# Recurrent attention and a squareplus layer: logarithms one group ahead, separate second-layer banks, crossbar transposes for row blocks 12 to 23

## Chip, cores and metric

The kernel runs on one core of a Trainium2 chip. The metric is the device time of one execution in microseconds (us). Engines are named as in the profile: PE (TensorE), DVE (VectorE), ACT (ScalarE), POOL (GpSimd) and SP, whose queue issues the DMAs here.

## What is computed

A gated linear attention with 4 batches, 8 heads, 768 steps and 48 features a head, followed by a two-layer network with 384 inputs and 2048 hidden units over the 3072 tokens:

```python
f = 1.0 / (1.0 + np.exp(-f_logit))
for t in range(S):
    state = f[:, :, t, :, None] * state + np.einsum('bhd,bhe->bhde', k[:, :, t], v[:, :, t])
    y[:, :, t] = np.einsum('bhd,bhde->bhe', q[:, :, t], state)
x = y.transpose(0, 2, 1, 3).reshape(B * S, H * D)
h = x @ w_in
g = 0.5 * (h + np.sqrt(h * h + 4.0))
out = g @ w_out
```

All inputs and the output are float32.

## The kernel before

**Units.** The 768 steps of a batch are six chunks of 128, so there are 24 *row blocks* of 128 tokens. Two row blocks make a *pair* (12 pairs), the unit of loading and of the first layer. `GROUPS` (L18) joins pairs to *groups* of 1, 1, 1, 2, 3, 3 and 1 pairs.

**Loads.** `load_pair` (L96) issues eight DMAs of 192 KB on SP for a pair: two row blocks each of f_logit, q, k and v. Each of the four kinds has four buffers, so a load waits until the pair four before it has been used up. The weights come in eight DMAs of 768 KB (L113, L119) and are cast to fp16 on ACT (w_in) and DVE (w_out).

**The window of a group** (`window`, L125) turns logits into scaled q and k. `exp_ln` (L131): ACT computes ln(1+exp(-f)) in two passes (L134, L135), DVE splits it into an fp16 part `lhi` (L137) and an fp16 remainder `llo` (L138), POOL casts v (L140). There are two buffers of lhi and llo. `cums` (L143): PE multiplies lhi and llo with a triangular matrix into the banks `hps` (L148, L149), ACT takes the exponentials `ea` and `eap` (L155, L156), POOL multiplies q and k by them into fp16 `qt` and `kt` (L157, L158), PE sums over half chunks (L164, L165), and DVE copies these sums to `nls` (L166). `gammas` (L168): DVE adds neighbouring sums to `gi` (L180), and ACT takes the decay from chunk to chunk, `gam` (L183). `run_window` (L366) puts an activation table load before and after this (exp and ln on one side, square root on the other).

**Attention of a row block**, in steps: `st_T` (L201) transposes q and k on PE, eight 128x128 tiles into a bank `tr`, and DVE copies them to `qkT` (L208). `st_SC` (L211) forms the scores of 8 heads in two banks and masks them on DVE (`pm`, L220). `st_KV` (L224) updates the state (`sn`, L235). `st_Y` (L239) forms y, which DVE casts (L251). `st_YT` (L254) transposes y on PE, three tiles, and DVE copies it into the pair's `xT` (L261). `attention` (L264) lays the steps of a group out in slots: transposes of its i-th row block in slot 4i, scores in 4i+2, state in 4i+3, y in 4i+5, y transposed in 4i+8.

**The two layers.** `mlp1` of a pair (L288) has eight halves of twelve matmuls (two by 256 columns, L299 six at a time) into the four `hps` banks; after every second half ACT squares (L306) and takes the root (L307), and DVE writes g (L310). `mlp2` (L317) has eight *quarters* of four matmuls (L328) into a bank `o`; after the fourth, DVE copies o to `o_sb` (two buffers, L332) and SP stores it (L334).

**Order.** ACT keeps the program's order. On the other engines a compile-time scheduler picks, by its own model of time, what is ready, earlier instructions in the program first; at run time every engine is in order. `run_mlp1` (L376) spreads the slots of attention over the halves, and takes quarters of the second layer from the list `fill` only when no slots are left or the list is longer than 24. `run_window` takes two quarters after each of its steps. The window of a group stands before mlp1 of the group before it.

**PSUM.** Four banks `hps`, and a pool of four, `pp_a`, that attention and o share.

Of the kernel before, what the change touches and what calls it, by code (L numbers as in the profile page):

```python
# [8 lines left out]
FP32 = mybir.dt.float32  # L9
# [5 lines left out]

GROUPS = [(0, 2), (2, 4), (4, 6), (6, 10), (10, 16), (16, 22), (22, 24)]  # L18
# [3 lines left out]
def kernel(  # L22
# [10 lines left out]
    nc = tc.nc  # L33
# [23 lines left out]
    pp_a = ctx.enter_context(tc.tile_pool(name="pp_a", bufs=4, space=PSUM))  # L57
# [20 lines left out]
    qt = [konst.tile([128, PR, H, 64], FP16, name=f"qt{i}") for i in range(NB)]  # L78
    kt = [konst.tile([128, PR, H, 64], FP16, name=f"kt{i}") for i in range(NB)]
    lhi = [konst.tile([128, PR, H, 64], FP16, name=f"lhi{i}") for i in range(2)]  # L80
    llo = [konst.tile([128, PR, H, 64], FP16, name=f"llo{i}") for i in range(2)]
# [14 lines left out]
    def load_pair(p):  # L96
        got = {}
        for name, src in (("f", f_logit), ("q", q), ("k", k), ("v", v)):
            t = ldp.tile([128, PR, H, D], FP32, name=f"ld_{name}", tag=f"ld_{name}")
            got[name] = t  # L100
        for name, src in (("f", f_logit), ("q", q), ("k", k), ("v", v)):
            for r in range(PR):
                b, c = divmod(p * PR + r, NC)
                nc.sync.dma_start(out=got[name][:, r],  # L104
                                  in_=src[b][:, c * C:(c + 1) * C, :].rearrange("h t d -> t h d"))
        loads[p] = got
# [18 lines left out]
    def window(g):  # L125

        r0, r1 = GROUPS[g]
        pairs = range(r0 // PR, r1 // PR)
        lss, steps = {}, []

        def exp_ln(p):  # L131
            f = loads[p]["f"]
            ls = wp.tile([128, PR, H, D], FP32, name="ls", tag="ls")
            nc.scalar.activation(out=f, in_=f, func=AF.Exp, scale=-1.0)  # L134
            nc.scalar.activation(out=ls, in_=f, func=AF.Ln, bias=1.0, scale=1.0)  # L135
            hi, lo = lhi[p % 2], llo[p % 2]
            nc.vector.tensor_copy(out=hi[:, :, :, 0:D], in_=ls)  # L137
            nc.vector.tensor_tensor(out=lo[:, :, :, 0:D], in0=ls, in1=hi[:, :, :, 0:D], op=ALU.subtract)  # L138
            v16 = bp.tile([128, PR, H, D], FP16, name="v16", tag="v16", bufs=4)
            nc.gpsimd.tensor_copy(out=v16, in_=loads[p]["v"])  # L140
            v16s[p] = v16

        def cums(p):  # L143
            hi, lo = lhi[p % 2], llo[p % 2]
            hp2 = [hps[2 * (p % 2) + r] for r in range(PR)]
            for r in range(PR):
                ca = hp2[r][:, 0:H * D]
                nc.tensor.matmul(out=ca, lhsT=wcent, rhs=hi[:, r, :, 0:D], start=True, stop=False)  # L148
                nc.tensor.matmul(out=ca, lhsT=wcent, rhs=lo[:, r, :, 0:D], start=False, stop=True)  # L149
            ea = wp.tile([128, PR, H, D], FP32, name="ea", tag="ea")  # L150
            eap = wp.tile([128, PR, H, D], FP32, name="eap", tag="eap")
            ld = loads[p]
            for r in range(PR):
                ca = hp2[r][:, 0:H * D]
                nc.scalar.activation(out=ea[:, r].rearrange("p h d -> p (h d)"), in_=ca, func=AF.Exp, scale=-1.0)  # L155
                nc.scalar.activation(out=eap[:, r].rearrange("p h d -> p (h d)"), in_=ca, func=AF.Exp, scale=1.0)  # L156
            nc.gpsimd.tensor_tensor(out=qt[p % NB][:, :, :, 0:D], in0=ld["q"], in1=ea, op=ALU.mult)  # L157
            nc.gpsimd.tensor_tensor(out=kt[p % NB][:, :, :, 0:D], in0=ld["k"], in1=eap, op=ALU.mult)  # L158
            b, c = divmod(p * PR, NC)
            for r in range(PR):  # L160
                nl = hp2[r][:, H * D:H * D + 2 * NP].rearrange("p (j s) -> p j s", s=2)
                for hp in range(NP):
                    o = nl[:, hp, :]
                    nc.tensor.matmul(out=o, lhsT=hi[:, r, 2 * hp:2 * hp + 2, :], rhs=hvec, start=True, stop=False)  # L164
                    nc.tensor.matmul(out=o, lhsT=lo[:, r, 2 * hp:2 * hp + 2, :], rhs=hvec, start=False, stop=True)  # L165
                nc.vector.tensor_copy(out=nls[b % 2][:, c + r], in_=nl)  # L166

        def gammas():  # L168

            a = r0  # L170
            while a < r1:
                b, c = divmod(a, NC)
                e = min(r1, (b + 1) * NC)
                n = e - a
                nb, gm = nls[b % 2], gam[b % 2]
                c0 = max(c - 1, 0)
                c1 = c + n - 1
                if c1 > c0:
                    gi = wp.tile([128, NC, NP], FP32, name="gi", tag="gi")
# [9 lines left out]
        for i, p in enumerate(ps):  # L189
            if i + 1 < len(ps):  # L190
                steps.append(lambda p=ps[i + 1]: exp_ln(p))
            steps.append(lambda p=p: cums(p))
# [260 lines left out]
```

## Time and profile before

| | |
|---|---|
| median of 3 runs | 272.44 us (270.02 to 272.85) |
| profiled execution, its own time | 270.39 us |
| its span, first to last instruction | 268.6 us |
| mean granted PE clock | 0.929 |
| DMA, all queues | 30.22 MB in 107032 packets, of which 100352 are under 512 B |
| POOL busy | 57.5 us |

The span is what the trace covers; the 1.8 us to the execution's own time lie outside it. "Busy" counts an engine's instructions and not its waits. Matmuls overlap, so the busy time of PE is more than its work. A line of the timeline reads: start, length, engine, line of the code, operation, output<-inputs, and in brackets the idle time before it and what ended that. In the table of stages each row is one stretch of the span. Numbers after the bar in a group's row are its busy time, the mean ns of one instruction, and idle time with its releaser.

### The profile page before, as it was taken

The page shows a single profiled execution, that of the slowest core. Times are in us where ns is not written, and L with a number is a line of the kernel's source. Part 1 is how long each engine was busy: PE and PEld are TensorE (multiplying, and loading weights), DVE is VectorE, ACT ScalarE, POOL GpSimd, SP SyncE. Part 2 cuts the span into 40 slices and gives each one's busy share as a digit, 9 for nine tenths or more (in the row PEclk, how much of TensorE's full clock was granted, in tenths as well). Part 3 has the DMA queues.
Part 4 walks back from the last instruction along what each step waited for, and adds up shares of the span by engine and source line. Part 5 has one row for each costly group of instructions (what it writes and reads, how often), then busy time and mean ns, then how long its engine had stood idle before and what let it go on. Part 6 is the DMA issues. An engine that isn't in the chain of part 4 may idle for free.

```text
span 268.6 us, 5160 instructions
## 1 busy us (share of the span) xinstructions
PE 213.1 (79%) x2024; PEld 148.9 (55%) x2024; DVE 182.7 (68%) x332; ACT 169.3 (63%) x252; POOL 57.5 (21%) x52
## 2 busy tenths in 40 slices
PE   0366939897688775986886869999886999999995
PEld 0143626664446553575664537777654777767652
DVE  1456726863583899579999666999983697645521
ACT  4355567884822956548968645988867795938200
POOL 4325001004209001494110396000005000000000
PEclk9999995999555997999999989999998899999999
DMA  8995599599995099999994000000000000010121
GB/s 144 187 220 184 161 234 302 153 245 188 177 216 93 8 214 185 187 217 195 166 199 76 31 32 29 2 0 4 2 29 29 2 29 33 29 59 32 59 79 70
DMA packets 107032, 30.22 MB, mean 113 GB/s; under 512 B 100352, under 2 KB 105472, under 8 KB 107008
## 3 DMA queue, kind: packets, MB, share of 16 engines
q1 hardware_dynamic: 107008, 29.89, 58.8%
q8 instruction: 16, 0.26, 0.4%
q14 instruction: 8, 0.07, 0.1%
HBM read 25.17 MB, written 4.72 MB: 111 GB/s over the span
## 4 chain that ended last, share of the span: by engine, by line
PE 32%; DVE 22%; ACT 16%; DMA 10%; issue 8%; SPq 6%; POOL 4%; POOLq 1%; ACTq 0%; DVEq 0%
PE o L328 16%; PE hps L299 10%; SPq L104 6%; DVE g L310 6%; ACT hsq L306 4%; DVE pm L220 3%; ACT r L307 3%; DMA ld_v<-in_v_dram 3%; DMA ld_f<-in_f_logit_dram 3%; DMA w_st<-in_moe_w_in_dram 3%; DVE qkT L208 2%; DVE llo L138 2%; POOL kt L158 2%; DVE y L251 2%; ACT L371 2%
## 5 line engine op out<-in xcount | busy, mean ns | idle before, releaser
L299 PE MATMUL hps<-xT,w_in 128*128 128x256 f16 x576 | 80.5, 285 | 10.6 <-DVE g L310 9.7
L310 DVE SCALAR_TENSOR_TENSOR g<-hps,r 128x512 f16<-128x512 f32 x96 | 61.8, 682 | 20.5 <-ACT r L307 20.5
L328 PE MATMUL o<-w_out,g 128*128 128x384 f16 x384 | 73.0, 335 | 0.2 <-DVE w_out L120 0.2
L299 PEld LDWEIGHTS <-w_in 128*128 128x128 f16 x576 | 57.0, 102 | 23.5 <-issue 13.2
L306 ACT ACTIVATE hsq<-hps 128x512 f16<-128x512 f32 x96 | 54.5, 590 | 23.4 <-PE hps L299 22.3
L307 ACT ACTIVATE r<-hsq 128x1024 f16<-128x1024 f16 x48 | 50.7, 1057 | 1.5
L328 PEld LDWEIGHTS <-g 128*128 128x128 f16 x384 | 37.6, 100 | 23.4 <-issue 3.3
L157 POOL TENSOR_TENSOR qt<-ld_q,ea 128x768 f16<-128x768 f32 x12 | 22.7, 1892 | 82.4 <-ACT ea L155 72.6
L220 DVE TENSOR_TENSOR pm<-sc,mask 128x512 f16<-128x512 f32 x48 | 30.9, 682 | 4.2 <-PE sc L218 4.2
L155 ACT ACTIVATE ea<-hps 128x384 f32<-128x384 f32 x24 | 11.9, 494 | 29.1 <-PE hps L149 29.1
L140 POOL CAST v<-ld_v 128x768 f16<-128x768 f32 x12 | 10.2, 853 | 65.6 <-DMA ld_v<-in_v_dram 60.7
L332 DVE COPY o_sb<-o 128x384 f32<-128x384 f32 x24 | 13.2, 554 | 16.0 <-PE o L328 16.0
L158 POOL TENSOR_TENSOR kt<-ld_k,eap 128x768 f16<-128x768 f32 x12 | 22.4, 1866 | 0.0
L208 DVE COPY qkT<-tr 128x1024 f16<-128x1024 f16 x24 | 16.4, 682 | 8.8 <-PE tr L206 8.8
L205 PE MATMUL tr<-ident,qt 128*128 128x128 f16 x96 | 16.7, 245 | 4.6 <-POOL qt L157 3.8
L206 PE MATMUL tr<-ident,kt 128*128 128x128 f16 x96 | 16.3, 246 | 4.7 <-POOL kt L158 4.7
L218 PE MATMUL sc<-qkT 48*128 48x128 f16 x192 | 12.1, 243 | 7.2 <-DVE qkT L208 7.1
L166 DVE COPY nls<-hps 128x8 f32<-128x8 f32 x24 | 3.8, 163 | 19.6 <-PE hps L165 18.6
L148 PE MATMUL hps<-lhi,wcent 128*128 128x384 f16 x24 | 8.2, 394 | 10.4 <-DVE wcent L66 8.7
L248 PE MATMUL y<-v,pm 128*128 128x48 f16 x192 | 14.1, 193 | 2.7 <-DVE pm L220 2.5
L183 ACT ACTIVATE gam<-gi 64x8 f32<-64x8 f32 (+2 forms) x18 | 3.8, 209 | 17.5 <-DVE gi L180 17.4
L206 PEld LDWEIGHTS <-kt 128*128 128x128 f16 x96 | 10.6, 111 | 7.5 <-POOL kt L158 5.8
(49 smaller groups left out, 256.0 us busy)
## 6 DMA issues: line engine op xcount, KB each, us to landing
ld_f<-in_f_logit_dram SPq DMA_DIRECT2D x24, 192.0 KB, 4.6
ld_q<-in_q_dram SPq DMA_DIRECT2D x24, 192.0 KB, 4.6
ld_k<-in_k_dram SPq DMA_DIRECT2D x24, 192.0 KB, 4.6
ld_v<-in_v_dram SPq DMA_DIRECT2D x24, 192.0 KB, 4.6
out_dram<-o_sb SPq DMA_DIRECT2D x24, 192.0 KB, 1.9
w_st<-in_moe_w_in_dram SPq DMA_DIRECT2D x4, 768.0 KB, 6.2
w_st<-in_moe_w_out_dram SPq DMA_DIRECT2D x4, 768.0 KB, 5.3
```

What stands on the lines that cost most here:

```text
L104: nc.sync.dma_start(out=got[name][:, r], in_=src[b][:, c * C:(c + 1) * C, :].rearrange("h t d -> t h d"))
L157: nc.gpsimd.tensor_tensor(out=qt[p % NB][:, :, :, 0:D], in0=ld["q"], in1=ea, op=ALU.mult)
L158: nc.gpsimd.tensor_tensor(out=kt[p % NB][:, :, :, 0:D], in0=ld["k"], in1=eap, op=ALU.mult)
L205: nc.tensor.transpose(out=tr[:, j, :], in_=qt[p % NB][:, i, 2 * j:2 * j + 2, :], identity=ident16)
L206: nc.tensor.transpose(out=tr[:, NP + j, :], in_=kt[p % NB][:, i, 2 * j:2 * j + 2, :], identity=ident16)
L208: nc.vector.tensor_copy(out=qkT, in_=tr)
L220: nc.vector.tensor_tensor(out=pm[:, s], in0=sc, in1=mask16.unsqueeze(1).broadcast_to([128, NP, C]), op=ALU.mult)
L299: nc.tensor.matmul(out=hb[:, a, :], lhsT=w_in16[:, j, jn * 128:(jn + 1) * 128], rhs=x[:, j, :], start=(j == 0), stop=(j == NJ - 1))
L306: nc.scalar.activation(out=hsq[:, a, :], in_=hps[(2 * j4 + a) % 4], func=AF.Square, scale=1.0)
L307: nc.scalar.activation(out=r16, in_=hsq, func=AF.Sqrt, scale=0.25, bias=1.0)
L310: nc.vector.scalar_tensor_tensor(out=g16[:, jn:jn + 2, :].rearrange("p a t -> p (a t)"), in0=hps[(2 * j4 + a) % 4], scalar=0.5, in1=r16[:, ...
L328: nc.tensor.matmul(out=o, lhsT=gts[p][:, jn, i * C:(i + 1) * C], rhs=w_out16[:, jn, :], start=(jn == 0), stop=(jn == NN - 1))
```

## The change

- `GROUPS` becomes 1, 1, 1, 1, 2, 2, 2 and 2 pairs.
- `exp_ln` becomes `logs`, which runs in the window of the group before; `lhi` and `llo` have four buffers. The llo subtraction moves from DVE to POOL, the cast of v from POOL to DVE (now in `decays`), the addition for gi from DVE to POOL.
- A window first runs `decays` for all its pairs, then `logs` of the next group, then `gammas`. After each pair's part it takes two quarters of the second layer and, from the fifth group's window on, two slots of attention.
- `run_mlp1` spreads only 80% of the slots (`SHARE`), except in the last group.
- f is loaded up to three groups ahead and q, k, v up to two.
- `pp_a` has two banks, and o has its own pool `pp_o` of two.
- q and k of a pair lie in one tile `qk`. For row blocks 12 to 23, one DMA transpose of [128, 1024] fp16 on SP's queue fills qkT (three buffers now), and one of [128, 384] fills the row block's part of xT. PE and DVE do nothing for these steps then.

```diff
+XBAR_FROM = 12
-GROUPS = [(0, 2), (2, 4), (4, 6), (6, 10), (10, 16), (16, 22), (22, 24)]
+GROUPS = [(0, 2), (2, 4), (4, 6), (6, 8), (8, 12), (12, 16), (16, 20), (20, 24)]
+SHARE = 0.8
...
-    pp_a = ctx.enter_context(tc.tile_pool(name="pp_a", bufs=4, space=PSUM))
+    pp_a = ctx.enter_context(tc.tile_pool(name="pp_a", bufs=2, space=PSUM))
+    pp_o = ctx.enter_context(tc.tile_pool(name="pp_o", bufs=2, space=PSUM))
...
+    NL = 4
+    qk = [konst.tile([128, PR, 2, H, 64], FP16, name=f"qk{i}") for i in range(NB)]
+    qt = [t[:, :, 0] for t in qk]
+    kt = [t[:, :, 1] for t in qk]
+    lhi = [konst.tile([128, PR, H, 64], FP16, name=f"lhi{i}") for i in range(NL)]
+    llo = [konst.tile([128, PR, H, 64], FP16, name=f"llo{i}") for i in range(NL)]
...
+    def logs(p):
+        f = loads["f", p]
+        ls = wp.tile([128, PR, H, D], FP32, name="ls", tag="ls")
+        nc.scalar.activation(out=f, in_=f, func=AF.Exp, scale=-1.0)
+        nc.scalar.activation(out=ls, in_=f, func=AF.Ln, bias=1.0, scale=1.0)
+        hi, lo = lhi[p % NL], llo[p % NL]
+        nc.vector.tensor_copy(out=hi[:, :, :, 0:D], in_=ls)
+        nc.gpsimd.tensor_tensor(out=lo[:, :, :, 0:D], in0=ls, in1=hi[:, :, :, 0:D], op=ALU.subtract)
+
+    def decays(p):
...
+        nc.gpsimd.tensor_tensor(out=qt[p % NB][:, :, :, 0:D], in0=loads["q", p], in1=ea, op=ALU.mult)
+        nc.gpsimd.tensor_tensor(out=kt[p % NB][:, :, :, 0:D], in0=loads["k", p], in1=eap, op=ALU.mult)
+        v16 = bp.tile([128, PR, H, D], FP16, name="v16", tag="v16", bufs=4)
+        nc.vector.tensor_copy(out=v16, in_=loads["v", p])
...
+                nc.gpsimd.tensor_tensor(out=gi[:, c0:c1], in0=nb[:, c0:c1, :, 1],
+                                        in1=nb[:, c0 + 1:c1 + 1, :, 0], op=ALU.add)
...
+        qkT = bp.tile([128, 2 * NP, C], FP16, name="qkT", tag="qkT", bufs=3)
+        if r < XBAR_FROM:
...
+        else:
+            nc.sync.dma_start_transpose(out=qkT, in_=qk[p % NB][:, i].rearrange("p a h d -> p (a h d)"))
...
+        xo = xTs[p][:, :, i * C:(i + 1) * C]
+        if r < XBAR_FROM:
...
+        else:
+            nc.sync.dma_start_transpose(out=xo, in_=part[r]["y16"].rearrange("p a b -> p (a b)"))
...
-                    box["o"] = pp_a.tile([128, DM], FP32, name="o", tag="a")
+                    box["o"] = pp_o.tile([128, DM], FP32, name="o", tag="o")
...
+    def window(g, g_logs, per=2, slots=1):
         nc.scalar.preload_act_table_set("natural_log_exp_and_others")
+        for p in pairs_of[g]:
+            decays(p)
+            for _ in range(slots):
+                att_slot()
             fill_some(per)
+        for h in g_logs:
+            for p in pairs_of[h]:
+                logs(p)
+                for _ in range(slots):
+                    att_slot()
+                fill_some(per)
+        gammas(g)
         nc.scalar.preload_act_table_set("sqrt_and_others")
         att.extend(attention(g))
+        loads_upto(pairs_of[min(g + 3, NG - 1)][-1] + 1, pairs_of[min(g + 2, NG - 1)][-1] + 1)
+
+    def run_mlp1(g, share):
+        natt = int(len(att) * share)
...
+    loads_upto(1, 1)
+    loads_upto(2, 2)
+    nc.scalar.preload_act_table_set("natural_log_exp_and_others")
+    logs(0)
+    decays(0)
+    gammas(0)
+    logs(1)
+    decays(1)
+    gammas(1)
...
+    run_mlp1(1, 1)
+    window(2, [3], 2, 0)
     while att:
         att_slot()
         fill_some(2)
+    window(3, [4], 2, 0)
+    run_mlp1(2, SHARE)
     for g in range(3, NG):
         if g + 1 < NG:
+            window(g + 1, [g + 2] if g + 2 < NG else [], 2, 2)
+        run_mlp1(g, SHARE if g + 1 < NG else 1)
     while fill:
         fill_some(1)
```

More of the change, by code (lines that the diff above doesn't have):

```diff
@@ L77 @@
     NB = 4
[L78 to L81, printed above, removed]
+    NL = 4
[4 more added lines that the diff above has]
+    llo = [konst.tile([128, PR, H, 64], FP16, name=f"llo{i}") for i in range(NL)]
     gam = [konst.tile([128, NC, NP, 2], FP32, name=f"gam{i}") for i in range(2)]
@@ L123 @@
     v16s = {}
-    def window(g):
-        r0, r1 = GROUPS[g]
[L128 to L179, printed above, removed]
-                    nc.vector.tensor_tensor(out=gi[:, c0:c1], in0=nb[:, c0:c1, :, 1],
-                                            in1=nb[:, c0 + 1:c1 + 1, :, 0], op=ALU.add)
-                    for s in range(2):
-                        nc.scalar.activation(out=gm[64 * s:64 * s + 64, c0:c1, :, s],
-                                             in_=gi[64 * s:64 * s + 64, c0:c1], func=AF.Exp, scale=-1.0)
-                a = e
-        ps = list(pairs)
-        steps.append(lambda p=ps[0]: exp_ln(p))
[L189 to L192, printed above, removed]
-        steps.append(gammas)
-        return steps
```

117 lines of the change are left out of this document (73 added, 44 removed).

## Prediction

> **What bounds the kernel now.** I read the head of the page first: no engine is full on average over the span.
>
> ```profile
> PE 213.1 (79%) x2024; PEld 148.9 (55%) x2024; DVE 182.7 (68%) x332; ACT 169.3 (63%) x252; POOL 57.5 (21%) x52
> ```
>
> Averages hide the stages, so next comes the table of busy times by stage. I cut it where ScalarE (ACT) loads an activation table: a stage of logarithms and exponentials (a window) begins with one load and ends with another, and the first-layer work (mlp1) lies between. After the stretch and its length stand the busy us of PE, weight loads, VectorE (DVE), ACT and GpSimd (POOL), the granted clock, the DMA share and GB/s.
>
> ```profile
> 0.00:58.30 58.30, 35.96 (x304) 24.59 (x305) 30.80 (x63) 35.28 (x48) 12.59 (x23) 0.94 0.98 204
> 58.30:68.30 10.00, 7.67 (x58) 4.29 (x56) 5.29 (x10) 6.30 (x11) 4.39 (x3) 0.92 1.40 188
> 68.30:89.00 20.70, 16.77 (x146) 11.12 (x147) 12.64 (x23) 9.56 (x17) 8.69 (x6) 0.55 0.87 147
> 89.00:100.60 11.60, 8.46 (x116) 6.62 (x115) 11.15 (x23) 8.53 (x12) 0.00 (x0) 1.00 0.63 126
> 100.60:123.40 22.80, 17.43 (x192) 11.80 (x194) 18.61 (x33) 13.07 (x26) 13.36 (x9) 0.93 1.22 196
> 123.40:144.50 21.10, 17.05 (x219) 13.18 (x219) 20.51 (x39) 17.23 (x25) 2.35 (x3) 1.00 1.19 179
> 144.50:166.20 21.70, 17.36 (x158) 10.78 (x160) 15.41 (x26) 12.94 (x24) 12.36 (x7) 0.92 0.08 28
> 166.20:196.00 29.80, 27.46 (x336) 21.95 (x334) 29.28 (x55) 26.49 (x38) 0.19 (x1) 1.00 0.01 2
> 196.00:206.00 10.00, 6.66 (x61) 4.05 (x58) 5.90 (x12) 6.26 (x10) 3.56 (x2) 1.00 0.11 39
> 206.00:268.60 62.60, 58.25 (x447) 40.56 (x447) 33.07 (x56) 33.68 (x49) 0.01 (x1) 0.97 0.12 42
> ```
>
> In order these are: the start with two one-pair windows and mlp1 of pairs 0 and 1; the window of pair 2; the window of pairs 3 and 4; mlp1 of pair 2; the window of 5 to 7; mlp1 of 3 and 4; the window of 8 to 10; mlp1 of 5 to 7; the window of pair 11; the rest (mlp1 of 8 to 11 and the second layer that is left). Three regimes stand out. DMA is full until about 145 us but for the slices around 89. The mlp1 stages are bound by DVE (20.51 of 21.1, 29.28 of 29.8). The last 62.6 us are bound by TensorE (PE: 58.25). In the windows nothing is full: three pairs take 22.8 and 21.7 us with ACT busy for 13. The reason stands in ACT's own timeline of the smallest window:
>
> ```profile
> 197.28 0.84 ACT L134 ACTIVATE ld_f<-ld_f 128x768 f32<-128x768 f32 x1
> ...
> 201.06 0.49 ACT L155 ACTIVATE ea<-hps 128x384 f32<-128x384 f32 x1 [2.06 <-PE hps L149]
> ...
> 204.30 0.43 ACT L183 ACTIVATE gam<-gi 64x8 f32<-64x8 f32 x2 [1.61 <-DVE gi L180]
> 204.75 1.28 ACT L371 ACT_TABLE_LOAD   x1
> ```
>
> Between logarithm and exponential ACT waits 2.06 us for the round trip DVE (split into hi and lo), PE (cumulative sums), and another 1.61 us for gi. With several pairs these waits add up.
>
> **Logarithms one group ahead.** The split of a group is done a window earlier, so at a window's start PE can form the sums at once and ACT runs 1.28 of table load, then four exponentials a pair (201.06 to about 202.7, 1.6 us), then two logarithm steps a pair for the next group (2 x 0.84), with no wait. But gi and the lo split move to POOL, which also multiplies q and k:
>
> ```profile
> 202.44 1.80 POOL L157 TENSOR_TENSOR qt<-ld_q,ea 128x768 f16<-128x768 f32 x1 [36.05 <-ACT ea L155]
> ```
>
> POOL's first multiply starts 1.38 us after the first exponential, 2.7 us into the window. Two pairs are four multiplies of 1.8: POOL is free 9.9 to 10.5 us in. If gi then goes first (0.3, estimated: 16 elements beside 768), the gammas (0.43 and a hand-off of 0.2) and the closing load (1.28) end the window at 12.5; if the two lo splits go first (same form as qt, 1.8 each), at 16.2. No such order on POOL is in this trace. The nearest row is DVE's:
>
> ```profile
> 153.44 0.76 DVE L180 TENSOR_TENSOR gi<-nls 128x8 f32<-128x8 f32 x1
> 154.17 0.56 DVE L332 COPY o_sb<-o 128x384 f32<-128x384 f32 x1
> 154.64 1.73 DVE L137 CAST lhi<-ls 128x768 f16<-128x768 f32 x1
> ```
>
> There a gi is executed ahead of a split that stands before it in the program, so what is ready first goes first. I take 13.2 a window, nearer to the first end. The cast took 1.73 us here, while POOL multiplied; the view of its tile has the spread (minimum, median and maximum in ns):
>
> ```profile
> L137 DVE CAST lhi<-ls x12: 547/556/2060, 6.8 to 199.0; 128x768 f16<-128x768 f32 x12
> L138 DVE TENSOR_TENSOR llo<-ls,lhi x12: 945/954/2441, 7.4 to 199.6; 128x768 f16<-128x768 f32 x12
> ```
>
> Afterwards the lo split has left DVE (12 x 0.95 at least) and the v cast has come, priced as the lhi cast: 12 of 0.55 to 2.06, 7 to 25 us, inside windows, where DVE has 5 us and more to spare.
>
> **What each stage then takes.** The start: the lo split costs 0.85 more twice, gammas of pair 0 now wait for kt on POOL (1.2), two table loads of 1.28 go: +0.7, 59.0. The window of pair 2 keeps its 10.0: its lo follow-up stands where the wait was. The next window holds pair 3 alone but needs f of pair 5:
>
> ```profile
> 69.43 1.84 SPq L104 DMA_DIRECT2D ld_f<-in_f_logit_dram  x2
> ...
> 79.92 1.25 SPq L104 DMA_DIRECT2D ld_q<-in_q_dram  x1
> 93.00 0.36 SPq L334 DMA_DIRECT2D out_dram<-o_sb  x1
> ```
>
> and by the page's list of DMA issues (the last number is us to landing)
>
> ```profile
> ld_f<-in_f_logit_dram SPq DMA_DIRECT2D x24, 192.0 KB, 4.6
> ...
> out_dram<-o_sb SPq DMA_DIRECT2D x24, 192.0 KB, 1.9
> ```
>
> Issued by 71.3 and landed 4.6 later, 75.9; two logarithm steps, gammas and table load end it near 80: 11 us in place of 20.7, because pair 4 is no longer in it. (Bounds: 9 without the wait, 20.7 if the queue is parked behind a store as from 81.2 to 93.0 here.) mlp1 of pair 2 now carries the attention of one pair, not two: DVE's 11.15 falls under ACT's floor, 9.5.
>
> Then four windows (pairs 4 to 11) of 13.2: 52.8, where three windows took 22.8 + 21.7 + 10.0 = 54.5 for pairs 5 to 11. Bounds 4 x 12 and 3 x 16.5 + 13.
>
> **The crossbar and the separate banks.** For row blocks 12 to 23 PE loses 12 x 11 transposes and DVE 12 copies of each of these two:
>
> ```profile
> 179.96 0.34 DVE L261 COPY xT<-yt 128x384 f16<-128x384 f16 x1
> 180.22 0.68 DVE L208 COPY qkT<-tr 128x1024 f16<-128x1024 f16 x1
> 180.82 0.54 DVE L251 CAST y<-y 128x384 f16<-128x384 f32 x1
> ```
>
> The two copies take 0.86 us by start times (179.96 to 180.82). In that stage DVE spent 29.28 us on six row blocks, 4.9 each; without the copies 4.0. The next limit is ACT:
>
> ```profile
> 214.40 1.07 ACT L306 ACTIVATE hsq<-hps 128x512 f16<-128x512 f32 x2
> 215.50 1.06 ACT L307 ACTIVATE r<-hsq 128x1024 f16<-128x1024 f16 x1
> 216.46 1.07 ACT L306 ACTIVATE hsq<-hps 128x512 f16<-128x512 f32 x2
> ```
>
> A step of 1024 columns comes every 2.06 us, eight to two pairs: 16.5, or 4.1 a row block. So mlp1 of two pairs with xbar rows takes 18 (16.5 to 19.9, the last being today's 29.8 x 2/3). mlp1 of pair 3 alone carries 80% of four PE-transposed rows: of the stage's 29.28 us, 24 of the g below (61.8 / 96 = 0.64 each) are 15.4, which leaves 2.3 of attention a row block; eight g and 3.2 row blocks are 5.1 + 7.4 = 12.5, and with first scores that wait I take 14.5 (at most 3.2 x 4.9 = 15.7).
>
> ```profile
> L310 DVE SCALAR_TENSOR_TENSOR g<-hps,r 128x512 f16<-128x512 f32 x96 | 61.8, 682 | 20.5 <-ACT r L307 20.5
> ```
>
> The sum for pairs 3 to 7 is 14.5 + 18 + 18 = 50.5, against 21.1 + 29.8 = 50.9. The gain is small because the work per pair of mlp1 moved, not only its price.
>
> The price of a transfer is nowhere in the trace. 256 KB (q and k) and 96 KB (y) a row block. Lower bound: as the output store, 1.9 us each. Upper: 32-byte pieces at the loads' price per packet,
>
> ```profile
> q1 hardware_dynamic: 107008, 29.89, 58.8%
> ```
>
> 0.588 x 268.6 x 16 / 107008 = 0.0236 us, so (8192 + 3072) / 16 x 0.0236 = 16.6 us a row block. I take loads of 192 KB as nearest: 4 to 5 us for qkT, 2 to 3 for y. That is hidden: qkT has three buffers, so its transfers run ahead of the scores as soon as POOL has written qk, and the loads that would stand before it end near 145 (the DMA share is 0.08 after that). It stops being hidden when a row block needs more than (13.2 + 18) / 4 = 7.8 us. Uncovered at each group's first row it would cost about 3 us, three times. The 24 issues go on SP's queue, past the last loads and the output stores; a store that waits for its o_sb holds them.
>
> By the Trainium skill, VectorE: DVE Perf Modes, section The three transpose paths, a 128x128 tile takes 1309 ns through the crossbar; eleven tiles in turn would be an estimated 14.4 us a row block, beyond the point of hiding, and the last three groups would grow by about 26 us each, to some 340 us. Advanced Engine Details and Errata, section X-Bar Transpose (TRN2), says instead that transposes are as fast as other DMAs, which is the forecast. No run here shows either yet.
>
> Two banks kept for o take two from attention; o held one or two of four before. I cost that at nothing, with up to 4 us inside mlp1's bound if PE then waits for DVE.
>
> **The rest.** In the program's order the second layer is filled in by quarters. After the last window 44 of 96 quarters are done, as now:
>
> ```profile
> 206.00:268.60 62.60, 37.04 (x208) 20.49 (x208) 0.97 0.12 42
> ```
>
> (208 of L328's 384 matmuls, so 52 quarters, are left.) So the rest costs what it does now, plus attention of two more row blocks (20 and 21), 1.7 us of PE each, estimated from the page's row of the scores:
>
> ```profile
> L218 PE MATMUL sc<-qkT 48*128 48x128 f16 x192 | 12.1, 243 | 7.2 <-DVE qkT L208 7.1
> ```
>
> (12.1 / 24 = 0.5, and y and the state update at a little more each): 66.0, bounds 62.6 to 69.
>
> **Sum.** 59.0 + 10.0 + 11.0 + 9.5 + 52.8 + 50.5 + 66.0 = 258.8 us, against 268.6. Outside the span lie 1.8 us (profiled execution 270.39), so 260.6. The median of the runs is 272.44, 2.05 above that execution; I give 262, between 260.6 and the same gain taken from the median.
>
> **Rivals.**
> A, POOL becomes the windows' bound: the lo splits go ahead of gi, as the program's order has them. Windows of 16.5, 16.5, 16.5 and 13, and 2 more in the window of pair 3: +11.7, so 272 to 274, no change. For it: both are ready before POOL is free. Against: the DVE rows above.
> B, the slower side: the crossbar moves small pieces. At 16.6 us a row block, four rows take 66 and a group 31.2: 35 more in each of three groups, near 365; decided at 7.8 us a row block. For it: 192-byte loads already take most of the DMA time. Against: the DMA engines are nearly idle from 145 us on.
> C, everything that is freed counts: the window of pair 3 in 9, windows of 12, mlp1 at 14.4 and twice ACT's 16.5, the rest at 62.6: 59.0 + 10.0 + 9.0 + 9.5 + 48.0 + 47.4 + 62.6 + 1.8 = 247. For it: ACT's waits for PE fall away wholly. Against: the rest is bound by PE, which then has more to do.
> D, the change doesn't get its logarithms ahead: a store parks SP as at 81.2 to 93.0, f of pairs 6 and 7 or a transpose comes 10 us late, ACT and then all else waits: 270. For it: the 11.8 us that SP stood still there. Against: fewer quarters of the second layer lie ahead of that store.
>
> **Chances.** Forecast 0.42, A 0.19, B 0.13, C 0.17, D 0.09 (half of it within 1%, half slower). A measurement of this kernel tells about 1% from no change. Faster by over 1%: forecast, C and a little of A, 0.63; within 1%: 0.18; slower: B, part of D and of A, 0.19. The range runs from C's 247 up past A and D to 280; it leaves out B and what lies under C.
>
> **What would show it.** Right: windows of 12 to 14 us for two pairs in ACT's timeline with no wait for hps between the logarithms and the exponentials; gi on POOL before the last lo; DVE no longer full in mlp1 from pair 4 on (17 of 18 us or less); transposes landing in under 5 us with nobody waiting long for qkT or xT; about 66 us after the last window. Wrong: ACT's gam waiting 3 us or more for POOL in each window (A); scores waiting for qkT DMA throughout (B); ACT or SP parked 10 us around 80 to 100 us (D).

## Result and the profile after

| | before | after |
|---|---|---|
| median of the runs | 271.25 us (270.02 to 272.85) | 257.9 us (255.22 to 258.54) |
| profiled execution | 270.39 us | 257.61 us |
| its span | 268.6 us | 255.8 us |
| mean granted PE clock | 0.929 | 0.92 |

The ratio is 0.9486, with a 95% interval of 0.9392 to 0.958: faster by about 5%. It is the ratio of the means of the four runs of each. Some executions took 1.5 to 2.1% longer than the fastest of their kernel, at a lower granted clock; the ratios leave them out, and the profiled execution of experiment 3 is one of them. The forecast was 262 us. The total came out close, but several terms of the sum did not.

The head of the page after (busy us, share of the span, number of instructions): DVE lost 17.7 us, POOL gained 13.3, PE lost the 132 transposes.

```profile
PE 209.0 (82%) x1892; PEld 147.2 (58%) x1892; DVE 165.0 (64%) x303; ACT 168.1 (66%) x252; POOL 70.8 (28%) x61
```

The table by stage, cut at the table loads as before, with the same columns:

```profile
0.00:60.00 60.00, 37.85 (x310) 26.83 (x311) 33.38 (x68) 34.48 (x48) 15.88 (x25) 0.94 1.02 209
60.00:68.80 8.80, 6.32 (x61) 3.59 (x58) 6.18 (x9) 6.21 (x11) 6.01 (x4) 1.00 1.31 188
68.80:78.10 9.30, 7.53 (x94) 5.68 (x93) 8.38 (x15) 7.96 (x12) 5.71 (x4) 0.85 0.37 90
78.10:93.00 14.90, 12.53 (x111) 9.05 (x110) 11.18 (x21) 8.57 (x13) 1.64 (x1) 0.86 1.07 182
93.00:105.40 12.40, 9.50 (x102) 6.44 (x101) 6.47 (x14) 9.29 (x16) 9.79 (x7) 1.00 1.12 181
105.40:117.70 12.30, 12.03 (x110) 8.49 (x108) 9.68 (x18) 8.67 (x13) 1.42 (x1) 0.72 1.07 198
117.70:130.40 12.70, 11.29 (x139) 8.14 (x138) 10.49 (x22) 9.43 (x17) 10.04 (x6) 1.00 0.87 152
130.40:148.40 18.00, 14.89 (x103) 10.78 (x103) 10.32 (x17) 16.76 (x24) 1.73 (x2) 0.91 1.30 197
148.40:161.00 12.60, 10.19 (x106) 6.35 (x105) 7.81 (x16) 9.62 (x19) 9.88 (x8) 0.99 0.20 53
161.00:188.00 27.00, 26.00 (x255) 19.04 (x254) 22.48 (x40) 17.15 (x25) 1.42 (x1) 0.82 0.36 70
188.00:199.70 11.70, 8.12 (x100) 5.90 (x99) 4.84 (x13) 6.17 (x13) 7.28 (x5) 0.94 0.44 93
199.70:255.80 56.10, 52.73 (x420) 36.91 (x418) 33.77 (x57) 33.77 (x48) 0.00 (x0) 0.95 0.19 53
```

Beside the prediction, stage by stage:

| stage | predicted | measured | off by |
|---|---|---|---|
| start, with pairs 0 and 1 | 59.0 | 60.0 | +1.0 |
| window of pair 2, window of pair 3 | 10.0 + 11.0 | 8.8 + 9.3 | -2.9 |
| mlp1 of pair 2 | 9.5 | 14.9 | +5.4 |
| four windows of two pairs | 4 x 13.2 = 52.8 | 12.4 + 12.7 + 12.6 + 11.7 = 49.4 | -3.4 |
| mlp1 of pair 3 | 14.5 | 12.3 | -2.2 |
| mlp1 of pairs 4 and 5 | 18 | 18.0 | 0 |
| mlp1 of pairs 6 and 7 | 18 | 27.0 | +9.0 |
| the rest | 66.0 | 56.1 | -9.9 |
| sum | 258.8 | 255.8 | -3.0 |

Against the kernel before, the windows went from 10.0 + 20.7 + 22.8 + 21.7 + 10.0 = 85.2 us to 67.5 (-17.7), mlp1 of pairs 2 to 7 from 11.6 + 21.1 + 29.8 = 62.5 to 72.2 (+9.7), the rest from 62.6 to 56.1 (-6.5), and the start from 58.3 to 60.0 (+1.7). That is -12.8, the difference of the two spans. So the gain lies in the windows and at the end, and mlp1 gave more than half of the windows' part back.

A window of two pairs in ACT's timeline (start, length, instruction, idle time before it with its releaser):

```profile
92.99 1.28 ACT L369 ACT_TABLE_LOAD   x1
94.28 0.49 ACT L151 ACTIVATE ea<-hps 128x384 f32<-128x384 f32 x1
...
99.93 0.84 ACT L134 ACTIVATE ls<-ld_f 128x768 f32<-128x768 f32 x1
103.67 0.44 ACT L182 ACTIVATE gam<-gi 64x16 f32<-64x16 f32 x2 [2.89 <-POOL gi L179]
104.13 1.28 ACT L382 ACT_TABLE_LOAD   x1
```

The first exponential follows the table load at once, so the round trip through DVE and PE is gone. What ACT waits for now is gi (2.60 to 2.89 us in three of the four windows of two pairs, 5.48 in the last), and POOL's timeline of the same window says why:

```profile
101.34 2.12 POOL L154 TENSOR_TENSOR qk<-ld_k,eap 128x768 f16<-128x768 f32 x1
103.42 0.22 POOL L179 TENSOR_TENSOR gi<-nls 128x16 f32<-128x16 f32 x1
103.60 3.23 POOL L137 TENSOR_TENSOR llo<-ls,lhi 128x768 f16<-128x768 f32 x2
```

gi takes 0.22 us and goes ahead of both lo splits, but after all four multiplies.

The transposes themselves were fast. From the view of the tile qkT (ns of one issue on SP: minimum, median, maximum; then us to landing):

```profile
L201 SPq DMA_TRANSPOSE qkT<-qk x12: 1231/1237/2097, 141.2 to 202.8; - x12
...
DMA to landing us min/median/max: 3.0/3.3/5.6
```

The 96 KB one of y landed in 2.3 us. But the first of qkT was issued at 141.2, although qk of its pair was written by 124.3. SP's timeline shows what stood ahead of it:

```profile
122.14 2.13 POOL L154 TENSOR_TENSOR qk<-ld_k,eap 128x768 f16<-128x768 f32 x1
```

```profile
127.58 2.32 SPq L331 DMA_DIRECT2D out_dram<-o_sb  x2
129.99 1.18 SPq L109 DMA_DIRECT2D ld_q<-in_q_dram  x2
...
139.02 2.03 SPq L109 DMA_DIRECT2D ld_v<-in_v_dram  x2
141.15 5.23 SPq L201 DMA_TRANSPOSE qkT<-qk  x3
146.58 4.89 SPq L331 DMA_DIRECT2D out_dram<-o_sb  x2
```

Two stores that waited for their results stood there, and twelve loads of q, k and v of the last two pairs. The consequence is in the table by stage restricted to the scores (L211; PE busy, weight loads busy, clock, DMA share, GB/s):

```profile
130.40:148.40 18.00, 0.00 (x0) 0.00 (x0) 0.91 1.30 197
148.40:161.00 12.60, 1.17 (x16) 0.73 (x16) 0.99 0.20 53
161.00:188.00 27.00, 4.84 (x46) 2.82 (x47) 0.82 0.36 70
```

mlp1 of pairs 4 and 5, which should have carried most of the attention of row blocks 12 to 15, ran without any, and mlp1 of 6 and 7 got it: 27 us with PE busy for 26.

The queue is not the whole delay. The slowest of the twelve transposes landed in 5.6 us, so the first had landed by 146.8, but the first scores start at 156.75. PE does not stand waiting for it: up to the scores it runs the second layer, and in the whole execution the scores wait for a transpose once.

```profile
153.25 3.57 PE L325 MATMUL o<-w_out,g 128*128 128x384 f16 x21
156.75 0.41 PE L211 MATMUL sc<-qkT 48*128 48x128 f16 x8
```

```profile
PE sc L211 <- DMA qkT<-qk: 2.5, 1, 2.5
```

So the other ten us are the place that the scores have in PE's order, which is fixed when the program is compiled. What time the scheduler reckoned for a transpose, no run shows.

Last, the second layer's matmuls after the last window, with the same columns:

```profile
199.70:255.80 56.10, 31.50 (x165) 15.72 (x163) 0.95 0.19 53
```

165 of 384 are left, where 208 were left before.

### The profile page after: what moved, and what is told of

Read it like the earlier page. It is cut to its first block, busy times and chain, and to the rows that moved or that the text cites. A ratio compares the mean times of both kernels' runs of the same rounds, so it can differ in the third digit from the quotient of the medians.

```text
span 255.8 us, 4975 instructions
## 1 busy us (share of the span) xinstructions
PE 209.0 (82%) x1892; PEld 147.2 (58%) x1892; DVE 165.0 (64%) x303; ACT 168.1 (66%) x252; POOL 70.8 (28%) x61
## 2 busy tenths in 40 slices
DMA packets 124696, 34.54 MB, mean 135 GB/s; under 512 B 118016, under 2 KB 123136, under 8 KB 124672
## 4 chain that ended last, share of the span: by engine, by line
PE 40%; ACT 15%; issue 13%; POOL 12%; DVE 8%; DMA 5%; SPq 3%; POOLq 1%; ACTq 0%; DVEq 0%
PE hps L296 18%; PE o L325 14%; POOL qk L154 4%; POOL qk L153 4%; ACT hsq L303 4%; ACT r L304 3%; SPq L109 3%; DVE g L307 3%; PE sc L211 3%; DMA w_st<-in_moe_w_in_dram 3%; POOL llo L137 2%; DMA ld_f<-in_f_logit_dram 2%; DVE pm L213 2%; ACT eap L152 1%; ACT w_in L118 1%
## 5 line engine op out<-in xcount | busy, mean ns | idle before, releaser
L325 PE MATMUL o<-w_out,g 128*128 128x384 f16 x384 | 79.2, 333 | 0.0
L296 PEld LDWEIGHTS <-w_in 128*128 128x128 f16 x576 | 59.0, 105 | 26.2 <-issue 12.4
L153 POOL TENSOR_TENSOR qk<-ld_q,ea 128x768 f16<-128x768 f32 x12 | 22.2, 1853 | 102.3 <-ACT ea L151 60.3
L211 PE MATMUL sc<-qkT 48*128 48x128 f16 x192 | 19.6, 243 | 9.3 <-DVE sn L228 4.4
L137 POOL TENSOR_TENSOR llo<-ls,lhi 128x768 f16<-128x768 f32 x12 | 19.8, 1657 | 24.2 <-DVE lhi L136 24.1
L154 POOL TENSOR_TENSOR qk<-ld_k,eap 128x768 f16<-128x768 f32 x12 | 23.3, 1938 | 0.0
L211 PEld LDWEIGHTS <-qkT 48*128 48x128 f16 x192 | 11.3, 103 | 17.8 <-issue 11.1
L329 DVE COPY o_sb<-o 128x384 f32<-128x384 f32 x24 | 13.2, 552 | 13.0 <-PE o L325 13.0
L182 ACT ACTIVATE gam<-gi 64x4 f32<-64x4 f32 (+3 forms) x18 | 3.8, 208 | 24.0 <-POOL gi L179 23.9
L228 DVE TENSOR_TENSOR sn<-u,gam 128x384 f16<-128x384 f32 x20 | 11.1, 553 | 10.0 <-ACT gam L182 7.6
L199 DVE COPY qkT<-tr 128x1024 f16<-128x1024 f16 x12 | 8.3, 691 | 10.8 <-PE tr L198 10.8
L241 PE MATMUL y<-v,pm 128*128 128x48 f16 x192 | 14.4, 200 | 1.0 <-DVE qkT L199 0.8
L136 DVE CAST lhi<-ls 128x768 f16<-128x768 f32 x12 | 10.6, 890 | 6.8 <-ACT ls L134 6.8
L244 DVE CAST y<-y 128x384 f16<-128x384 f32 x24 | 13.2, 549 | 2.3 <-PE y L241 2.3
```

Of the source, the lines that this page charges most:

```text
L137: nc.gpsimd.tensor_tensor(out=lo[:, :, :, 0:D], in0=ls, in1=hi[:, :, :, 0:D], op=ALU.subtract)
L153: nc.gpsimd.tensor_tensor(out=qt[p % NB][:, :, :, 0:D], in0=loads["q", p], in1=ea, op=ALU.mult)
L154: nc.gpsimd.tensor_tensor(out=kt[p % NB][:, :, :, 0:D], in0=loads["k", p], in1=eap, op=ALU.mult)
L211: nc.tensor.matmul(out=sc[:, j, :], lhsT=qkT[o:o + D, NP + j, :], rhs=qkT[o:o + D, j, :], start=True, stop=True)
L241: nc.tensor.matmul(out=y[:, j, s], lhsT=pm[:, s, j, :], rhs=v16s[p][:, i, 2 * j + s, :], start=(c == 0), stop=(c == 0 or s == 1))
L244: nc.vector.tensor_copy(out=y16.rearrange("p a b -> p (a b)"), in_=y.rearrange("p a b d -> p (a b d)"))
```

## Experiments

All ratios are to the kernel before, run beside each. Unless it says otherwise, an edit is made on the kernel after (0.9486).

**1. Logarithms in the group's own window.**

```diff
     def window(g, g_logs, per=2, slots=1):
...
-        for p in pairs_of[g]:
+        ps = pairs_of[g]
+        logs(ps[0])
+        for n, p in enumerate(ps):
+            if n + 1 < len(ps):
+                logs(ps[n + 1])
             decays(p)
-            for _ in range(slots):
+            for _ in range(2 * slots):
...
-        for h in g_logs:
-            for p in pairs_of[h]:
-                logs(p)
...
+            fill_some(2 * per)
...
-    logs(2)
```

> Logarithms in the group's own window again (POOL, banks, crossbar and groups as in the changed kernel; as many quarters and slots a window). Theory W (running the logarithms ahead is what shortens the windows): the way from the logarithm over DVE, POOL and PE to the exponential comes back; a window of two pairs takes 16 to 17 us instead of 12.5, that of one pair 2 more; 270 to 278 us. Theory P (PE and the second layer bound the kernel): 258 to 262 us.

Measured: 276.46 us, ratio 1.0151 (1.0083 to 1.0219). Of all single undoings this is the only one whose interval lies above 1. The six windows take 12.8, 16.9, 16.7, 18.4, 16.7 and 16.7, 98.2 us in place of 67.5; mlp1 (-8.8) and the rest (-3.4) give some back. In its view of waits (total us, times, longest us) the wait that was removed is there again, and the one for POOL has not gone:

```profile
ACT gam L182 <- POOL gi L179: 35.6, 9, 5.9
...
ACT ea L151 <- PE hps L146: 21.5, 8, 7.1
```

In the kernel after these are 23.9 and 8.3. The logarithms ahead are worth 1.0151 - 0.9486 = 0.067, some 18 us, more than the whole gain. That holds with the lo split and gi on POOL, as the change has them: the way from logarithm to exponential passes POOL here, where it passed DVE in the kernel before. No run has the logarithms late and these two on DVE.

**2. POOL in the program's order**, so that both lo splits go ahead of gi.

```diff
-    ctx.enter_context(tc.manual_schedule(engines={mybir.EngineType.Activation}))
+    ctx.enter_context(tc.manual_schedule(engines={mybir.EngineType.Activation, mybir.EngineType.Pool}))
```

> POOL kept to the program's order, so that the lo splits stand before gi in every window (rival A of the prediction, made on purpose). Theory W: ACT's wait for gi grows by 1.6 us in the window of pair 2 and 3.3 in each of the four that have two splits; windows of about 16 us; 266 to 271 us. Theory P (PE and the second layer bound the kernel, a longer window is filled with quarters): 257 to 261 us.

Measured: 269.4 us, 0.9866 (0.9806 to 0.9926). Its POOL at the end of the window of pair 3 and in that of pairs 6 and 7, and its waits:

```profile
85.52 1.64 POOL L137 TENSOR_TENSOR llo<-ls,lhi 128x768 f16<-128x768 f32 x1 [6.45 <-DVE lhi L136]
...
137.85 1.64 POOL L137 TENSOR_TENSOR llo<-ls,lhi 128x768 f16<-128x768 f32 x1 [0.50 <-DVE lhi L136]
139.99 1.88 POOL L137 TENSOR_TENSOR llo<-ls,lhi 128x768 f16<-128x768 f32 x1 [0.49 <-DVE lhi L136]
141.84 0.21 POOL L179 TENSOR_TENSOR gi<-nls 128x12 f32<-128x12 f32 x1
```

```profile
ACT gam L182 <- POOL gi L179: 45.1, 8, 10.4
```

Windows of 15.6, 16.7, 16.0 and 11.7, the one of pair 3 18.4, that of pair 2 10.6. Rival A was a true mechanism, and its total is near: +11.7 worked out, and 0.9866 - 0.9486 = 0.038, some 10 us, measured. But the windows grew by 21.6 us (67.5 to 89.1). The window of pair 3 alone grew by 9.1, because gi there also waits until DVE has cast the second lhi. mlp1 (-8.4) and the rest (-1.1) gave back nearly half. In the kernel after, the compiled order avoids all this.

**3. One pool of four banks again**, shared by attention and o.

```diff
-    pp_a = ctx.enter_context(tc.tile_pool(name="pp_a", bufs=2, space=PSUM))
-    pp_o = ctx.enter_context(tc.tile_pool(name="pp_o", bufs=2, space=PSUM))
+    pp_a = ctx.enter_context(tc.tile_pool(name="pp_a", bufs=4, space=PSUM))
...
-                    box["o"] = pp_o.tile([128, DM], FP32, name="o", tag="o")
+                    box["o"] = pp_a.tile([128, DM], FP32, name="o", tag="a")
```

> o takes its banks from attention's pool of four again. Theory W: 256 to 260 us, no change that can be told. Theory B (the separate banks keep PE from waiting for a bank, and are a good part of the gain): 263 us or more.

Measured: 267.86 us, 0.98 (0.974 to 0.9861). So the banks, which I had costed at nothing, are worth 0.031, 8.5 us by the ratios. The second layer's matmuls left after the last window:

```profile
204.50:268.40 63.90, 37.91 (x208) 20.36 (x208) 0.94 0.19 55
```

208 again, and 63.9 us of rest, 7.8 more than after. (The profiled execution took 270.64 us at a granted clock of 0.886. The count doesn't depend on that; the 63.9 may by a per cent.) The count is not the only effect: the window of pair 3 takes 14.1 in place of 9.3, because ACT waits 5.33 us for sums that PE's order has behind 14 matmuls of the second layer, the scores and the transposes of a row block.

**4. The separate banks in the kernel before**, and nothing else.

```diff
-    pp_a = ctx.enter_context(tc.tile_pool(name="pp_a", bufs=4, space=PSUM))
...
+    pp_a = ctx.enter_context(tc.tile_pool(name="pp_a", bufs=2, space=PSUM))
+    pp_o = ctx.enter_context(tc.tile_pool(name="pp_o", bufs=2, space=PSUM))
...
-                    box["o"] = pp_a.tile([128, DM], FP32, name="o", tag="a")
+                    box["o"] = pp_o.tile([128, DM], FP32, name="o", tag="o")
```

> The kernel before with nothing but the separate banks for o. The compiled order has 16 matmuls of the second layer more ahead of the last window than before (176 instead of 160 by the time that mlp1 of eight pairs is issued), so the end gets 16 x 0.164 = 2.6 us shorter. Theory Q (separate banks let quarters run ahead): 267 to 271 us. Theory N (two banks are too few for attention in this kernel): 273 us or more.

Measured: 271.77 us, 0.9994 (0.994 to 1.0047): nothing. Its last window ends at 210.7, and the second-layer matmuls left then are

```profile
210.70:269.30 58.60, 34.65 (x192) 18.45 (x192) 1.00 0.12 42
```

16 fewer than the 208 before, and the rest is 4.0 us shorter than the 62.6 there; but the last window ends 4.7 us later (206.0 before). Work only moved. My reading is that in the old order the stages had no holes for it, and that in the new one they have; the runs show the counts and the times.

**5. No crossbar.** `XBAR_FROM = 24`: every row block is transposed on PE and copied by DVE.

```diff
-XBAR_FROM = 12
+XBAR_FROM = 24
```

> All row blocks transposed by PE again, the rest as in the changed kernel. Theory W (the gain is the windows': logarithms ahead, smaller groups): PE gets 132 transposes back (7.4 us of PE) and DVE 24 copies (12.4 us), but the 7.5 us that ACT waits at 161 us, because the first transposes stand behind the last loads on SP, fall away. So 256 to 262 us. Theory X (the crossbar's relief of DVE and PE is the gain): 266 to 271 us, most of the gain gone.

Measured: 258.42 us, 0.9405 (0.9338 to 0.9472), which is not told apart from the 0.9486 of the kernel after. The two stages that differ, and its second-layer matmuls left:

```profile
160.20:179.90 19.70, 19.70 (x197) 14.74 (x197) 17.42 (x31) 17.29 (x25) 1.76 (x1) 0.91 0.01 4
```

```profile
191.90:253.90 62.00, 35.76 (x192) 18.45 (x192) 0.97 0.11 39
```

mlp1 of pairs 6 and 7 takes 19.7 in place of 27.0, and the rest 62.0 in place of 56.1. The crossbar takes 7.3 us in one place and gives 5.9 in another. In this pair of kernels DVE isn't the bound of that stage (22.48 of 27.0 with the crossbar, 17.42 of 19.7 with its copies); PE is busy for 26.00 and 19.70.

**6. The last loads one group later**, so that q, k and v of pairs 10 and 11 no longer stand ahead of the first transposes.

```diff
-        loads_upto(pairs_of[min(g + 3, NG - 1)][-1] + 1, pairs_of[min(g + 2, NG - 1)][-1] + 1)
+        loads_upto(pairs_of[min(g + 3, NG - 1)][-1] + 1, min(pairs_of[min(g + 2, NG - 1)][-1] + 1, 10))
...
         run_mlp1(g, SHARE if g + 1 < NG else 1)
+        loads_upto(12, 12 if g > 3 else 10)
```

> q, k and v of pairs 10 and 11 are asked for one group later, so that the transposes of row blocks 12 to 15 go out when POOL has written qk (124 us) and not behind those loads (141 us). If the queue's order is what makes ACT wait 7.5 us at 161 us: that wait falls to under 2 us and the stage that starts there from 27 to 19 to 21 us; the rest after the last window grows by 3 to 6 us, for PE has fewer quarters behind it then; 251 to 256 us. If the wait is hidden by PE's work anyway: 257 to 259 us, with the rest longer by as much as the stage is shorter.

Measured: 252.75 us, 0.9269 (0.9227 to 0.931). The first transposes go out 11.4 us earlier, the first scores 10.8 us earlier (145.99), and mlp1 of pairs 6 and 7 takes 19.9:

```profile
129.73 4.09 SPq L201 DMA_TRANSPOSE qkT<-qk  x3
```

```profile
161.60:181.50 19.90, 19.37 (x187) 13.52 (x184) 16.87 (x30) 16.85 (x24) 2.03 (x2) 1.00 0.62 117
```

So the 7 us go back to a place in SP's queue and not to the crossbar's speed. They came by way of PE's order, which moved with the issue: here too the scores start 16.3 us after it, against 15.6 in the kernel after.

**7. Crossbar from row block 6 on**, with the later last loads of experiment 6.

```diff
-XBAR_FROM = 12
+XBAR_FROM = 6
```

> Crossbar from row block 6 on, with the last loads one group later as in the run that had that alone (252.75 us). If a transpose is cheap wherever it stands: 250 to 253 us, PE and DVE being freer by another 4 and 6 us. If it has to wait in SP's queue behind loads that keep the DMA engines full until about 130 us: transposes of row blocks 6 to 11 land 5 us or more after they could be issued, scores wait for them, 255 to 262 us.

Measured: 269.4 us, 0.9907 (0.9863 to 0.995), worse than either expectation. mlp1 of pair 3 takes 29.0 and that of 4 and 5 24.8. A transpose still lands in 3.3 us (median), but in the half of the run where the loads are, its place in the queue is late. qk of pair 3 is written by 76.2, its transposes go out at 106.64 behind loads, and here PE does stand waiting for them:

```profile
74.39 1.81 POOL L154 TENSOR_TENSOR qk<-ld_k,eap 128x768 f16<-128x768 f32 x1
```

```profile
104.74 1.80 SPq L109 DMA_DIRECT2D ld_v<-in_v_dram  x2
106.64 3.31 SPq L201 DMA_TRANSPOSE qkT<-qk  x2
```

```profile
110.79 0.62 PE L211 MATMUL sc<-qkT 48*128 48x128 f16 x8 [12.88 <-DMA qkT<-qk]
```

**8. gi, the lo split and the cast of v back on the engines that had them.**

```diff
-        nc.gpsimd.tensor_tensor(out=lo[:, :, :, 0:D], in0=ls, in1=hi[:, :, :, 0:D], op=ALU.subtract)
+        nc.vector.tensor_tensor(out=lo[:, :, :, 0:D], in0=ls, in1=hi[:, :, :, 0:D], op=ALU.subtract)
...
-        nc.vector.tensor_copy(out=v16, in_=loads["v", p])
+        nc.gpsimd.tensor_copy(out=v16, in_=loads["v", p])
...
-                nc.gpsimd.tensor_tensor(out=gi[:, c0:c1], in0=nb[:, c0:c1, :, 1],
+                nc.vector.tensor_tensor(out=gi[:, c0:c1], in0=nb[:, c0:c1, :, 1],
```

> The lo split and gi on DVE and the cast of v on POOL, as before the change, all else as in the changed kernel. POOL has 19 us less to do, but none of it stood before gi; DVE has some 5 us more, mostly inside windows. Theory W: 256 to 261 us, no difference. If moving these to POOL was needed: 263 us or more.

Measured: 253.68 us, 0.9309 (0.9227 to 0.939), faster than expected. The same window as above, in ACT's timeline:

```profile
89.30 1.28 ACT L369 ACT_TABLE_LOAD   x1
...
96.12 0.84 ACT L134 ACTIVATE ls<-ld_f 128x768 f32<-128x768 f32 x1
96.87 0.43 ACT L182 ACTIVATE gam<-gi 64x16 f32<-64x16 f32 x2
97.32 1.28 ACT L382 ACT_TABLE_LOAD   x1
```

No wait is left in this window: it is 9.3 us of ACT's own work, 3.1 less than after. The other three of two pairs take 15.3, 9.7 and 8.1, where they took 12.7, 12.6 and 11.7. The one that grew is that of pairs 6 and 7: ACT waits 4.73 us for gi, which stands behind both lo splits on DVE. The window of pair 3 grew as well, from 9.3 to 13.1.

**9. gi alone back on DVE.**

```diff
-                nc.gpsimd.tensor_tensor(out=gi[:, c0:c1], in0=nb[:, c0:c1, :, 1],
+                nc.vector.tensor_tensor(out=gi[:, c0:c1], in0=nb[:, c0:c1, :, 1],
```

> gi alone back on DVE; the lo split stays on POOL and the cast of v on DVE. Theory G (gi stands behind POOL's four multiplies, and that wait is all that the engines' moves cost): windows of two pairs end some 3 to 4 us earlier (8.5 to 9.5 us), 253 to 256 us, as with all three moved back (253.68). Theory H (POOL's extra 20 us of lo splits are the cost): 257 to 260 us, as the changed kernel.

Measured: 255.06 us, 0.9406 (0.9353 to 0.9459). The windows of two pairs take 9.4, 14.6, 9.9 and 8.1, nearly those of experiment 8, so in three of the four it was gi's place on POOL that ended the window. In that of pairs 6 and 7 gi comes later on DVE than it did on POOL (ACT waits 4.51 us for it), and the window of pair 3 takes 15.2 in place of 9.3. In total the interval overlaps that of the kernel after, and mlp1 of pairs 6 and 7, with the first transpose still issued late (139.4), grew from 27.0 to 29.9.

**10. gi on DVE and the later last loads** (the edits of 9 and 6).

```diff
-                nc.gpsimd.tensor_tensor(out=gi[:, c0:c1], in0=nb[:, c0:c1, :, 1],
+                nc.vector.tensor_tensor(out=gi[:, c0:c1], in0=nb[:, c0:c1, :, 1],
...
+        loads_upto(12, 12 if g > 3 else 10)
```

> gi back on DVE, and the last loads one group later. If the two costs are separate places (windows; the wait at 161 us) they add: 247 to 251 us. If PE's remaining work takes most of it back: 251 to 254 us.

Measured: 250.15 us, 0.9233 (0.9168 to 0.9299), the fastest kernel here. The two savings, 5.2 and 2.8 us by the medians, very nearly add up: 7.8 was measured. Its interval is clear of that of the kernel after, but not of experiment 6's (0.9269) or 11's.

**11. All three engines back and the later last loads** (the edits of 8 and 6).

```diff
+        nc.vector.tensor_tensor(out=lo[:, :, :, 0:D], in0=ls, in1=hi[:, :, :, 0:D], op=ALU.subtract)
...
+        loads_upto(12, 12 if g > 3 else 10)
```

> The lo split and gi on DVE, the cast of v on POOL, and the last loads one group later. As the kernel with gi alone back, within 2 us: 246 to 251 us; the lo split costs DVE 0.95 us and POOL 1.65, neither on a path that ends a window.

Measured: 252.04 us, 0.9286 (0.9232 to 0.9341), the same as experiment 8 without the later loads and 1 us above what was expected. mlp1 of pairs 6 and 7 falls here too, from 27.4 to 19.8, but mlp1 of pair 3 (+1.8) and of pairs 4 and 5 (+3.3) and the rest (+2.1) take it back. What the later loads are worth depends on the order that they meet.

**12. All three engines back and no crossbar** (the edits of 8 and 5).

```diff
-XBAR_FROM = 12
+XBAR_FROM = 24
...
+        nc.vector.tensor_tensor(out=lo[:, :, :, 0:D], in0=ls, in1=hi[:, :, :, 0:D], op=ALU.subtract)
```

> The engines moved back and no crossbar. Against the kernel with both the engines back and the later loads this is the crossbar without its wait in the queue: PE has 132 transposes and their waits more, 26 fewer matmuls of the second layer fit in before the last window (178 for 191 at the eighth pair in the compiled order), 2 to 6 us slower than that kernel, 250 to 254 us. If a DVE that is no longer freed is what decides: 256 us or more.

Measured: 257.71 us, 0.9536 (0.9471 to 0.9601), in the range that was given for a DVE that decides (256 or more). Against experiment 8, which differs by the crossbar alone, the crossbar gains 0.023, some 6 us. The times themselves show less: 4.0 us between the medians, 2.9 between the profiled spans. The rest is 57.2 there with 165 matmuls of the second layer left, and 62.2 here with 193. These are 28 more; the 26 of the expectation and its "178 for 191", which makes 13, don't agree with each other. mlp1 of 6 and 7 takes 27.4 there and 24.0 here, and in these 24.0 DVE is busy for 21.65 and PE for 20.34, so DVE as the bound of that stage is not excluded. In the kernel after the same gain at the end is taken back by mlp1 of 6 and 7, which is 7.3 longer there with the crossbar, not 3.4.

## Why the prediction was right, and where it was wrong

**Right: the logarithms ahead.** The windows of two pairs came out at 11.7 to 12.7 where 13.2 was taken, by the mechanism named: ACT's first exponential follows its table load, and gi passes the lo splits on POOL. Experiment 1 shows that without it the whole gain is lost, with the engines as the change has them. The window of pair 3 (9.3) didn't wait for f of pair 5, for which 11 had been allowed.

**Right: that rival A would not come. Its price was near by cancelling.** Experiment 2 had to force it, and it then cost some 10 us. The 3.3 us more in a window with two lo splits was right (3.2 to 4.0 measured). The 2 in the window of pair 3 was 9.1, and mlp1 gave 8.4 back, which the price did not have.

**Right: a transfer's cost.** 3.3 and 2.3 us to landing, under the 4 to 5 and near the 2 to 3 that I took. Rival B did not happen: its 32-byte pieces were not there, for 4.32 MB in 17664 more packets is some 245 bytes a packet, an estimate from the two totals. By the Trainium skill, VectorE: DVE Perf Modes, section The three transpose paths, eleven tiles would have taken an estimated 14.4 us; here eight of them land in 3.3 us and three in 2.3. The Trainium skill's Advanced Engine Details and Errata, section X-Bar Transpose (TRN2), which says that transposes are as fast as other DMAs, agrees with this trace: a load of 192 KB lands in 4.5 to 4.7, a transpose of 256 KB in 3.3.

**Wrong: "That is hidden".** The step looked at how long a transfer takes and when DMA engines are free. It said that the loads ahead would end near 145 and that the transposes go past them, and then didn't charge it. What counts is when SP reaches the issue, 17 us after qk was there, and where PE's compiled order then has the scores, some ten us after the first transpose had landed. Then mlp1 of pairs 4 and 5 comes out at the 18.0 that I gave it, for a wrong reason: it carries no attention. The next one pays 27.0. Experiment 6 takes out 7 of the 9 us that I missed.

**Wrong: "After the last window 44 of 96 quarters are done, as now".** 165 matmuls were left, so 55 quarters were done. With 0.19 us for one (31.50 / 165), the 43 matmuls are 8.2 us of the 9.9 by which the rest was shorter. The cause is the term "I cost that at nothing": with o in the shared pool the count is 208 again (experiment 3). Banks matter to the compile-time order. My reading is that a quarter which needs a bank of attention's pool can't be placed until attention releases one, and with its own two fills holes of PE in the windows; the runs show the counts, and not the scheduler's reason. Experiment 4 shows that it takes the new order too. PE time that the crossbar frees lets more ahead as well: without it 192 are left (experiment 5).

**Not borne out: why the crossbar pays.** I let it relieve DVE, as the bound of mlp1. Experiment 5 has no crossbar and DVE is at 17.42 of 19.7 with PE full. That smaller groups and the attention moved into windows had already taken DVE from the bound is the likely reason, but no run undoes these. Where the crossbar's gain is seen is the end, where PE has fewer matmuls left: in experiments 8 and 12 it shortens the rest by 5.0 us (62.2 to 57.2). But in experiment 12 DVE is at 21.65 of 24.0 in mlp1 of pairs 6 and 7, so how much of the gain is PE's and how much DVE's stays open.

**Wrong size: mlp1 of pair 2.** ACT's floor of 9.5 was missed by 5.4. ACT waits 5.00 us in one piece:

```profile
87.95 0.60 ACT L303 ACTIVATE hsq<-hps 128x512 f16<-128x512 f32 x1 [5.00 <-PE hps L296]
```

PE's order has y, scores and the transpose of a row block in these 5 us, with gaps for DVE in between. In experiments 1 and 2 the stage took 10.0 and 10.2, with 8 and 0 matmuls of the scores in it in place of 16; but the window before it, which got them, took 16.9 and 18.4 in place of 9.3. No run changes this alone, so its cause is only argued.

**The start.** The terms given for it, 2 x 0.85 + 1.2 - 2 x 1.28, make +0.3 and not the +0.7 that went into the sum; it measured +1.7.

So the total came close by cancelling, which is luck: +9.0 and +5.4 against -9.9, -3.4, -2.9 and -2.2, with +1.0 at the start. A forecast that had put right only one of the two large terms would have been off by 12 or by 7 us of span, in place of 3.

**Open.** gi on DVE saves 2.7 to 3.6 us in three of the four windows of two pairs (experiment 9) and lengthens the other by 1.9 and that of pair 3 by 5.9; in total 0.9406 isn't told apart from 0.9486, and how much of it is real stays open. SP also stood still behind a store, as in rival D, from 70.3 to 78.9 us:

```profile
69.15 1.19 SPq L109 DMA_DIRECT2D ld_f<-in_f_logit_dram  x2
78.94 0.36 SPq L331 DMA_DIRECT2D out_dram<-o_sb  x1
```

The kernel's view of waits puts no long wait down to it, but no run took the store away. Nor does any run undo the smaller groups, `SHARE` or the earlier loads alone.

## To carry to other kernels

Where stages alternate on one engine, computing what the next stage needs first one stage earlier can be worth more than making any of its parts faster. A DMA transpose costs little to transfer, but it takes its turn in the issuing queue: write down what stands ahead of it there, waits included, before calling it hidden. Then look where the instruction that uses it stands in its engine's order, for a compiled order can hold it back after the data have landed. A background stream of matmuls should have banks of its own once there are holes for it to fill, and whether it runs ahead is read by counting what is left after the last stage.

## What the hardware showed that was not expected

- A crossbar transpose of 128x1024 fp16 in 3.0 us at the least and 3.3 in the middle, of 128x384 in 2.3; an issue holds SP for 1.24 us. 24 of them added 17664 packets (124696 against 107032) and 4.32 MB.
- A sum of 128x16 takes POOL 0.22 us, so its place in POOL's order costs more than its work: 2.89 us of waiting in one window, 10.4 at the longest where it stood last, behind two lo splits of which one waited for DVE (experiment 2).
- The lo split takes 1636 ns on POOL where DVE took 954 in the kernel before (medians).
